# Reordering the first tile: weight chunks against the second batch of keys and values

## The chip, the core and the metric

The kernel runs on one core of a Trainium2 chip. The metric is the device time of the core in microseconds (us), from the start of the program to its end. TensorE is PE in the profile, VectorE DVE, ScalarE ACT, GpSimd POOL; SyncE (SP) issues all transfers.

## What is computed

Three layers follow each other, on 8 batches of 8 heads, 576 positions, 64 dimensions per head, so 4608 tokens of 512 features. The first is a linear attention whose `k`-`v` product is a 64 by 64 matrix per head; the second a feed-forward layer with a rational function; the third a gated one. Cut to what matters here:

```python
kv  = einsum('bhsd,bhse->bhde', k, v)
out = einsum('bhsd,bhde->bhse', q, kv)
x   = out / sqrt(mean(out * out, -1) + 1e-6) * g_norm      # then tokens by 512
h   = x @ w_in                                             # 512 by 2048
g   = (a0 + a1*h + a2*h*h + a3*h*h*h) / (1 + |b0|*|h| + |b1|*h*h + 1e-6)
y   = g @ w_out                                            # 2048 by 512
# third layer: silu(y @ w_gate) * (y @ w_val) @ w_o2
```

All inputs are float32. Products of the two feed-forward layers are made as three matmuls of a high and a low part (`mm3`).

## The kernel before

**Tiles and steps.** Tokens are worked in 9 tiles of 512. In the second layer a tile takes 16 steps (`NF1`), one for each 128 of the 2048 hidden features; step `s` runs over all tiles, `t, f = divmod(s, NF1)`. On PE a step is `h_mm(s)` (12 matmuls, the hidden features of this step, into one of two PSUM banks `ph`), then `y_mm(s - 2)` (12 matmuls, what the step two earlier gives to the output), and now and then a matmul of the attention of the next tile (`attn_pe`: `po` or `ss`).

**The function of a step.** `g_step(s)` reads the bank `ph` with three ACT instructions and three DVE ones (tiles `e`); before its own DVE part it runs `g_finish(s - 1)`, three DVE instructions, after which ACT makes the high part of `ghl` and POOL the low part. `y_mm(s - 1)` waits for these. The bank `ph` of step `s`, which `h_mm(s + 2)` needs again, is free when the last DVE instruction of `g_step(s)` is done. In this document block `s` is what DVE does from the first instruction of `g_finish(s - 1)` to the start of the next block.

**Weight chunks.** In the first tile the 32 chunks of the second layer's weights (512 KB each) are also brought in and converted: 16 of `w_in` (here i0 to i15) and 16 of `w_out` (o0 to o15), in the order i0, i1, i2, o0, i3, o1, i4, o2 and so on, numbered 0 to 31. Chunk `n` ends in a tile `wt` that has the slot `w{n}`. A conversion takes a shift on DVE and a scaling on ACT (`w_scale`, both on `wraw`), a join on DVE, the high part on ACT (`w_hi`) and a subtraction on DVE (`wt<-wraw,wt`). The raw chunks lie in a ring of four tiles, so chunk `n` can be fetched when chunk `n - 4` has had its subtraction. ACT and DVE take their instructions in the order in which they are written, and so does SP with the transfers: an instruction that waits for a chunk holds what is behind it.

**Keys and values.** The 8 batches of keys and values (2.25 MB each, four loads `kvm` and one `kvr`) use slots of the same pool `w` before the `wt` tiles come to them. A batch's products on PE (`kv_mm`, four times) go into the bank `pkv` (`pa1`, there is one) and are copied out by ACT (`kvf` for the first two batches, `kvc` for the others). The first batch is multiplied while the first tile's `x` is made; the second follows, before step 0; the others stand in the steps 0, 3, 4, 7, 8 and 11 of tile 0, one each.

**The first tile before.** Ahead of step 0, chunk 0 is converted alone and chunks 1 and 2 as a pair; each step of tile 0 then converts two:

```python
            g_step(s, raws[:2] if t == 0 else raw_u[0][f - 3:f - 2] if t == TILES - 1 and 3 <= f < 5 else ())
            ...
            if t == 0:
                lows = wa_hi(len(raws[:2]))
                for w in raws[:2]:
                    w_scale(w)
                run(lows, 2)
                wa_fetch(2)
                kv_load(4, done)
```

The order of everything in this stage is written out by hand; no scheduler moves it.

Of the kernel before, what the change touches and what calls it, by code (L numbers as in the profile page):

```python
# [8 lines left out]
F32 = mybir.dt.float32  # L9
# [6 lines left out]
P = 128  # L16
# [7 lines left out]
NF1, NF2 = F1 // P, F2 // P  # L24
HP = H // 2
LAG = 2
WARM = 10
S1 = TILES * NF1
NP = 2
# [11 lines left out]
def fused_kernel(ctx: ExitStack, tc: tile.TileContext, kv_main, kv_left, q_t, w_in, w_out, w_gate, w_val, w_o2, ab, g_norm, out):  # L41
# [48 lines left out]
    def act(out, in_, func=AF.Copy, **kw):  # L90
        nc.scalar.activation(out=out, in_=in_, func=func, **kw)  # L91
# [95 lines left out]
    kv_jobs = [(b, hp) for b in range(B) for hp in range(HP)]  # L187
    kv_last = {}

    def kv_tag(n):  # L190
        slots = (24, 25, 28, 29, 30, 20, 21, 22, 23)
        return f"w{slots[n] if n < 5 else slots[(n - 5) % 9] if n < 28 else slots[n - 27]}"

    def kv_load(k, done=None):

        done = kv_n[1] if done is None else done
        for n in range(kv_n[0], min(kv_n[0] + k, len(kv_jobs))):
            b, hp = kv_jobs[n]
            tag = kv_tag(n)
            if kv_last.get(tag, -1) >= done or (b > 1 and done < n - hp - HP):  # L200
                return
            kv_last[tag] = n
            m = w_p.tile([P, 4, 2, P], F32, tag=tag, name="kvm")
            nc.sync.dma_start(out=m, in_=kv_main[b, hp])
            if hp == 0:
                r = w_p.tile([64, HP, 2, P], F32, tag=("w26", "w27")[b % 2], name="kvr")
                nc.sync.dma_start(out=r, in_=kv_left[b])
                kv_in[b] = r
            kv_in[b, hp] = m
            kv_n[0] += 1  # L210

    def kv_mm(ps):
        b, hp = kv_jobs[kv_n[1]]
        kv_n[1] += 1
        m, r = kv_in.pop((b, hp)), kv_in[b]
        for c in range(4):
            for j in range(2):
                nc.tensor.matmul(ps[diag(j), hp, diag(j)], lhsT=m[:, c, 0, diag(j)], rhs=m[:, c, 1, diag(j)], start=(c == 0), stop=False)
        for j in range(2):
            nc.tensor.matmul(ps[diag(j), hp, diag(j)], lhsT=r[:, hp, 0, diag(j)], rhs=r[:, hp, 1, diag(j)], start=False, stop=True)  # L220

    def diag(j):
        return slice(64 * j, 64 * j + 64)

    def kv_evac_first(b, ps, hps):
        for j in range(2):
            dst, src = kvf[diag(j), b, hps, diag(j)], ps[diag(j), hps, diag(j)]
            act(dst, src)

    def kv_evac(b, ps):  # L230
        for j in range(2):
            act(kvc[diag(j), b - 2, :, :], ps[diag(j), :, diag(j)])

    def kv_split(b):
        hi, lo = kvh[b % 2], kvl[b % 2]
# [170 lines left out]

    def g_step(s, joins=()):
        ps = ew.pop(s)
        attn_head(s)
# [4 lines left out]
        act(e2, ps, AF.Abs, scale=ab_raw[:, 4:5])  # L414
        act(e3, ps, AF.Identity, scale=na[:, 3:4], bias=na[:, 2:3])
# [12 lines left out]
        mid[s] = (e1, e2, e3)  # L428
# [340 lines left out]
    with tc.manual_schedule():  # L769
# [11 lines left out]
            elif i == 2:  # L781
                wa_fetch(1)
        nc.sync.dma_start(out=ab_raw, in_=ab.partition_broadcast(P))
        wa_fetch(1)
        kv_load(1)
        wa_fetch(1)
        nc.vector.memset(kvf, 0.0)
        nc.vector.memset(ones_b, 0.0)
        for j in range(2):
# [11 lines left out]
        def first(i, stage):  # L801
            if not 0 <= i < HP:
                return
            if stage == "kv":
                kv_mm(pkv)
                kv_evac_first(0, pkv, slice(i, i + 1))
                kv_load(1)
            elif stage == "out":
                po[i] = out_mm(0, i, ps_y.tile([P, N], F32, tag=f"y{i}", name="po"))
                sqs[i] = w_p.tile([P, N], F32, tag=f"w{8 + i}", name="sq")  # L810
                act(sqs[i], po[i], AF.Square)
            elif stage == "ss":
                pss[i] = ss_mm(0, sqs[i], ps_h.tile([P, N], F32, tag="ph", name="ss"))
                nb[i] = tuple(w_p.tile([P, N], F32, tag=f"w{k + i}", name="nb") for k in (12, 16))
                norm_start(0, pss[i], nb[i])
            elif stage == "norm":
                st["n"] = nb[i]
                ops = norm_ops(po[i], pss[i])
                run(ops, 3)
            else:  # L820
                st["n"] = nb[i]
                x_attn(0, i, nc.gpsimd)

        for i in range(HP + 2):
            if i == 1:
                nc.vector.tensor_scalar(out=g_neg, in0=g_raw, scalar1=-0.5 / D, scalar2=None, op0=ALU.mult)
            first(i, "kv")
            first(i - 1, "ss")
            first(i, "out")
            if i == 1:  # L830
                w_scale(raws[0])
            elif i == 2:
                w_join(raws[0])
            elif i == 3:
                wa_split(1)
            first(i - 1, "norm")
            first(i - 2, "x")
        nc.vector.tensor_scalar(out=na, in0=ab_raw[:, 0:4], scalar1=-1.0, scalar2=None, op0=ALU.mult)
        act(b_abs, ab_raw[:, 4:6], AF.Abs)
        pkv = ps_a.tile([P, HP, P], F32, tag="pa1", name="pkv")  # L840
        for i in range(HP):
            kv_mm(pkv)
            if i == 0:
                q_load(1, 0)
                wa_fetch(2)
        kv_evac_first(1, pkv, slice(0, HP))
        attn_pe(-1)
        for w in raws[:2]:
            w_scale(w)
        w_join(*raws[:2])  # L850
        lows = wa_hi(2)
        for w in raws[:2]:
            w_scale(w)
        run(lows, 2)
        kv_load(3)
        wa_fetch(2)
        kv_load(2)


        kv_b = None  # L860
        for s in range(S1):
            t, f = divmod(s, NF1)
            if s == S1 - NF1:
                attn_ctx.close()
                late["p"] = ctx.enter_context(tc.tile_pool(name="late", bufs=1, side="right", reuse_waits="tile"))
                u_fetch(0)
                u_fetch(1)
            done = kv_n[1]
            h_mm(s)
            if s >= LAG:  # L870
                y_mm(s - LAG)
            attn_pe(s)
            if t == TILES - 1 and f == 2:
                u_scale(0)
            if kv_b:
                kv_evac(*kv_b)
                kv_b = None
            if t == 0 and f in (0, 3, 4, 7, 8, 11):
                pkv = ps_a.tile([P, HP, P], F32, tag="pa1", name="pkv")
                kv_b = (kv_jobs[kv_n[1]][0], pkv)  # L880
                for _ in range(HP):
                    kv_mm(pkv)
            g_step(s, raws[:2] if t == 0 else raw_u[0][f - 3:f - 2] if t == TILES - 1 and 3 <= f < 5 else ())
            if s >= LAG and f == LAG - 1:
                y_evac((s - LAG) // NF1, s_p, "stg")
            attn_tail(s)
            if t == 0:
                lows = wa_hi(len(raws[:2]))
                for w in raws[:2]:
                    w_scale(w)  # L890
                run(lows, 2)
                wa_fetch(2)
                kv_load(4, done)
            if t == TILES - 1:
                if f == 5:
                    val[0] = [w_views(r)[2] for r in raw_u.pop(0)]
                    u_first(nc.gpsimd)
                elif f in (6, 7):
                    raw_x["D", f - 6] = y_fetch(0, f - 6, 0, N, s_p, "stg")
# [230 lines left out]
```

## Time and profile before

| | |
|---|---|
| time, median of 3 runs | 1732.32 us (1731.52 to 1733.18) |
| time of the profiled execution | 1728.57 us |
| its span, first to last instruction | 1726.8 us |
| PE busy in the span | 1702.2 us (99%) |
| DVE busy in the span | 1227.9 us (71%) |
| ACT busy | 1002.0 us (58%) |
| POOL busy | 460.5 us (27%) |
| HBM read, written | 117.44 MB, 57.67 MB |

Times inside the profile count from the start of the span. The profiled execution's time is 1.8 us above its span and 3.75 us below the median of the timed runs. Matmuls overlap, so the start of one and the start of the next tell more than their durations; "busy" of PE hides nothing but waits.

### The profile page before, as it was taken

The numbers are of one execution on the slowest core, as the hardware profiler recorded it, in microseconds if no ns is written. First come the engines' busy times: TensorE is split into PE (matmuls) and PEld (weight loads), VectorE is DVE, ScalarE is ACT, GpSimd is POOL, SyncE is SP. The second block draws the span as 40 slices with busy tenths as digits, with TensorE's granted clock in tenths as the row PEclk, the third lists the DMA queues.
The fourth block names the chain that finished last, engine by engine and source line by source line (L and its number), as shares of the span: only waits on it lengthen the run. The fifth ranks groups of instructions, "written<-read, shape, count | busy, mean of one in ns | idle before, by whom it ended". The sixth has DMA issues, their size and how long they took to land.

```text
span 1726.8 us, 21854 instructions
## 1 busy us (share of the span) xinstructions
PE 1702.2 (99%) x8112; PEld 1403.0 (81%) x8112; DVE 1227.9 (71%) x1657; ACT 1002.0 (58%) x1664; POOL 460.5 (27%) x331
## 2 busy tenths in 40 slices
PE   8999999999999999999999999999999999999999
PEld 5767888888888888888888888888888888888887
DVE  5989999999999999998886656666547666213211
ACT  6878787878778787877774434444334445112110
POOL 1223444444444343433322302222102212000000
PEclk9999999999999999999999999999999999999999
DMA  9771101000101010001107537222542355423411
GB/s 328 277 232 53 37 13 37 13 31 13 37 13 37 13 38 13 31 13 52 71 31 270 199 110 274 80 91 81 189 152 99 109 193 199 169 98 132 161 49 49
DMA packets 68682, 176.53 MB, mean 102 GB/s; under 512 B 7648, under 2 KB 10208, under 8 KB 66784
## 3 DMA queue, kind: packets, MB, share of 16 engines
q1 hardware_dynamic: 68576, 175.15, 28.8%
q8 instruction: 63, 1.03, 0.3%
q14 instruction: 43, 0.35, 0.1%
HBM read 117.44 MB, written 57.67 MB: 101 GB/s over the span
## 4 chain that ended last, share of the span: by engine, by line
PE 52%; issue 1%; DVE 0%; DMA 0%; POOL 0%; ACT 0%; SPq 0%; DVEq 0%; POOLq 0%; ACTq 0%
PE pb L105 10%; PE pb L106 10%; PE pb L107 10%; PE pb L757 6%; PE pb L759 6%; PE pb L758 6%; PE y L107 1%; PE y L105 1%; PE y L106 1%; PE ph L106 1%; PE ph L107 1%; PE ph L105 1%; DVE e L432 0%; DMA yraw<-yd 0%; POOL xc L94 0%
## 5 line engine op out<-in xcount | busy, mean ns | idle before, releaser
L94 POOL TENSOR_TENSOR ghl<-e,ghl 128x512 fp32r<-128x512 f32 x144 | 192.9, 1340 | 517.3 <-ACT ghl L91 229.0
L105 PE MATMUL pb<-xc,wu 128*128 128x512 f32 (+1 forms) x816 | 308.9, 378 | 1.1 <-DVE e L432 1.1
L106 PE MATMUL pb<-xc,wu 128*128 128x512 f32 (+1 forms) x816 | 308.6, 378 | 0.0
L107 PE MATMUL pb<-xc,wu 128*128 128x512 f32 (+1 forms) x816 | 308.6, 378 | 0.0
L101 DVE SCALAR_TENSOR_TENSOR e<-e,e 128x512 f32<-128x512 f32 x288 | 247.3, 859 | 30.8 <-ACT e L91 24.6
L106 PE MATMUL y<-ghl,wt 128*128 128x512 f32 x576 | 226.4, 393 | 6.3 <-POOL ghl L94 6.3
L105 PE MATMUL ph<-x,wt 128*128 128x512 f32 x576 | 227.8, 396 | 0.0
L105 PE MATMUL y<-ghl,wt 128*128 128x512 f32 x576 | 225.5, 391 | 2.3 <-ACT ghl L91 2.3
L107 PE MATMUL y<-ghl,wt 128*128 128x512 f32 x576 | 225.8, 392 | 0.0
L106 PE MATMUL ph<-x,wt 128*128 128x512 f32 x576 | 225.3, 391 | 0.1
L107 PE MATMUL ph<-x,wt 128*128 128x512 f32 x576 | 224.6, 390 | 0.0
L432 DVE TENSOR_TENSOR e<-e,pb 128x512 f32<-128x512 f32 (+1 forms) x192 | 124.5, 653 | 139.5 <-PE pb L107 85.4
L91 ACT ACTIVATE e<-pb 128x512 f32<-128x512 f32 (+1 forms) x144 | 82.2, 571 | 233.2 <-PE pb L107 232.9
L105 PEld LDWEIGHTS pb<-xc,wu 128*128 128x128 f32 x816 | 153.3, 188 | 30.4 <-DVE e L432 1.7
L107 PEld LDWEIGHTS pb<-xc,wu 128*128 128x128 f32 x816 | 153.3, 188 | 28.7
L106 PEld LDWEIGHTS pb<-xc,wu 128*128 128x128 f32 x816 | 153.3, 188 | 28.6
L757 PE MATMUL pb<-wo,xc 128*128 128x512 f32 x432 | 168.0, 389 | 0.0
L758 PE MATMUL pb<-wo,xc 128*128 128x512 f32 x432 | 168.0, 389 | 0.0
L759 PE MATMUL pb<-wo,xc 128*128 128x512 f32 x432 | 168.0, 389 | 0.0
L91 ACT ACTIVATE e<-ph 128x512 f32<-128x512 f32 x144 | 85.5, 594 | 117.2 <-PE ph L107 116.9
L378 DVE COPY sb<-pb 128x512 f32<-128x512 f32 x18 | 12.5, 692 | 197.9 <-PE pb L759 197.8
L101 DVE SCALAR_TENSOR_TENSOR e<-e,na,e 128x512 f32<-128x512 f32 x144 | 143.7, 998 | 0.0
(120 smaller groups left out, 3057.8 us busy)
## 6 DMA issues: line engine op xcount, KB each, us to landing
graw<-gd SPq DMA_DIRECT2D x108, 256.0 KB, 4.8
gd<-gout SPq DMA_DIRECT2D x84, 256.0 KB, 2.0
kvm<-in_kv_main SPq DMA_DIRECT2D x32, 512.0 KB, 9.3
yraw<-yd SPq DMA_DIRECT2D x26, 512.0 KB, 6.0
q<-in_q_t SPq DMA_DIRECT2D x36, 256.0 KB, 2.7
yd<-sb SPq DMA_DIRECT2D x18, 512.0 KB, 3.3
wraw<-in_w_in SPq DMA_DIRECT2D x16, 512.0 KB, 6.1
wraw<-in_w_out SPq DMA_DIRECT2D x16, 512.0 KB, 3.9
```

The costliest lines, as they stand in the source:

```text
L91: nc.scalar.activation(out=out, in_=in_, func=func, **kw)
L94: eng.tensor_tensor(out=out, in0=a, in1=b.bitcast(F32), op=ALU.subtract)
L101: nc.vector.scalar_tensor_tensor(out=out, in0=in0, scalar=scalar, in1=in1, op0=op0, op1=op1)
L105: nc.tensor.matmul(ps, lhsT=wh, rhs=xh, start=first, stop=False, skip_group_check=more)
L106: nc.tensor.matmul(ps, lhsT=wh, rhs=xl, start=False, stop=False, skip_group_check=more)
L107: nc.tensor.matmul(ps, lhsT=wl, rhs=xh, start=False, stop=last, skip_group_check=more)
L378: nc.vector.tensor_copy(out=sb[:, 1, :], in_=yps[2 * j + 1])
L432: eng.tensor_tensor(out=out, in0=a, in1=b, op=op)
L757: nc.tensor.matmul(b[m], lhsT=gh, rhs=w[:, 0, :], start=f == 0, stop=False)
L758: nc.tensor.matmul(b[m], lhsT=gh, rhs=w[:, 1, :], start=False, stop=False)
L759: nc.tensor.matmul(b[m], lhsT=gl, rhs=w[:, 0, :], start=False, stop=f == NF2 - 1)
```

## The change

Ahead of step 0 five chunks are converted instead of three, one at a time (`convert`), and their transfers are issued ahead of the second batch's. The products of the second batch are moved behind `h_mm(0)`, and the first attention matmuls of the second tile move one or two steps back. The batch that was multiplied in step 0 is multiplied in step 3; each later batch moves on by one place, and step 7 takes two (`kv_batches(2)`), copied out by one instruction. The function `pace` sets how many chunks a step converts: one in the steps 1, 2, 5 and 6, three in 8 and 9, two in the others. The transfer slots of keys and values are listed in a new table (`kv_slots`) in place of `kv_tag`.

```diff
+PRE = 5
-    def kv_evac(b, ps):
-        for j in range(2):
-            act(kvc[diag(j), b - 2, :, :], ps[diag(j), :, diag(j)])
+    def kv_batches(k):
+        ps = ps_a.tile([P, 2, HP, D], F32, tag="pa1", name="pkv")
+        b = kv_jobs[kv_n[1]][0]
+        for i in range(k):
+            for _ in range(HP):
+                kv_mm(lambda hp, j: ps[diag(j), i, hp, :])
+        return partial(act, kvc[:, b - 2:b - 2 + k, :, :], ps[:, :k])
...
-        wa_fetch(1)
+        wa_fetch(3)
         kv_load(1)
-        wa_fetch(1)
...
+        def convert():
+            w_scale(raws[0])
+            w_join(raws[0])
+            wa_split(1)
+            wa_fetch(1)
...
             elif i == 3:
                 wa_split(1)
+                wa_fetch(1)
+                q_load(1, 0)
             first(i - 1, "norm")
             first(i - 2, "x")
+            if i > 3:
+                convert()
...
-        pkv = ps_a.tile([P, HP, P], F32, tag="pa1", name="pkv")
-        for i in range(HP):
-            kv_mm(pkv)
-            if i == 0:
-                q_load(1, 0)
-                wa_fetch(2)
-        kv_evac_first(1, pkv, slice(0, HP))
-        attn_pe(-1)
+        for _ in range(PRE - 3):
+            convert()
         for w in raws[:2]:
             w_scale(w)
-        w_join(*raws[:2])
-        lows = wa_hi(2)
-        for w in raws[:2]:
-            w_scale(w)
-        run(lows, 2)
-        kv_load(3)
-        wa_fetch(2)
-        kv_load(2)
+        def pace(s):
+            return 1 if s in (1, 2, 5, 6) else 3 if s in (8, 9) else 2
+        scaled = 2
...
             h_mm(s)
+            if s in (1, 2):
+                attn_pe(2 * s - 3)
             if s >= LAG:
                 y_mm(s - LAG)
-            attn_pe(s)
+            if s == 0:
+                pkv = ps_a.tile([P, HP, P], F32, tag="pa1", name="pkv")
+                for _ in range(HP):
+                    kv_mm(kv_first(pkv))
+                kv_evac_first(1, pkv, slice(0, HP))
+                done = kv_n[1]
+            elif s > 2:
+                attn_pe(s)
...
-            if t == 0 and f in (0, 3, 4, 7, 8, 11):
-                pkv = ps_a.tile([P, HP, P], F32, tag="pa1", name="pkv")
-                kv_b = (kv_jobs[kv_n[1]][0], pkv)
-                for _ in range(HP):
-                    kv_mm(pkv)
-            g_step(s, raws[:2] if t == 0 else raw_u[0][f - 3:f - 2] if t == TILES - 1 and 3 <= f < 5 else ())
+            if t == 0 and f in (3, 4, 7, 8, 11):
+                kv_b = kv_batches(2 if f == 7 else 1)
+            if t == 0:
+                for w in raws[scaled:pace(s)]:
+                    w_scale(w)
+            g_step(s, raws[:pace(s)] if t == 0 else raw_u[0][f - 3:f - 2] if t == TILES - 1 and 3 <= f < 5 else ())
...
-                lows = wa_hi(len(raws[:2]))
-                for w in raws[:2]:
+                lows = wa_hi(len(raws[:pace(s)]))
+                k = len(lows)
+                scaled = min(len(raws), pace(s + 1))
+                for w in raws[:scaled]:
                     w_scale(w)
-                run(lows, 2)
-                wa_fetch(2)
+                run(lows, k)
+                wa_fetch(k)
+                attn_tail(s)
                 kv_load(4, done)
```

PE at the end of the first tile's attention, before: the last two of the second batch's four groups of products (`pkv`), the next tile's `po`, and then the first product of step 0 (`ph`).

```order
L218 MATMUL pkv<-kvm 64x64 x8
L220 MATMUL pkv<-kvr 64x64 x2
L218 MATMUL pkv<-kvm 64x64 x8
L220 MATMUL pkv<-kvr 64x64 x2
L256 MATMUL po<-q,kvf 128x64
L256 MATMUL po<-q,kvf 128x448
L105 MATMUL ph<-x,wt 128x512
```

And now, the same place:

```order
L267 MATMUL po<-q,kvf 128x512
L287 MATMUL ss<-sq,ones_b 128x512
L106 MATMUL ph<-x,wt 128x512
L107 MATMUL ph<-x,wt 128x512
L108 MATMUL ph<-x,wt 128x512
```

Step 0 follows the first tile's last `ss` at once; the second batch's products come behind its 12 matmuls, and `po` behind those of step 1.

DVE from the last instruction of the first tile's norm (`nb`) to the first of step 0 (`e`), before; `x2` is a pair of chunks:

```order
L101 SCALAR_TENSOR_TENSOR nb<-po,g_neg,nb 128x512
L838 TENSOR_SCALAR na<-ab_raw 128x4
L125 TENSOR_SCALAR wraw<-wraw 128x512 x2
L101 SCALAR_TENSOR_TENSOR wraw<-wraw 128x512 x2
L125 TENSOR_SCALAR wraw<-wraw 128x512 x2
L94 TENSOR_TENSOR wt<-wraw,wt 128x512 x2
L101 SCALAR_TENSOR_TENSOR wraw<-wraw 128x512 x2
L101 SCALAR_TENSOR_TENSOR e_559<-e_559,b_abs,e_560 128x512
```

And now, the last of the four single conversions and what follows it:

```order
L126 TENSOR_SCALAR wraw<-wraw 128x512
L102 SCALAR_TENSOR_TENSOR wraw<-wraw 128x512
L95 TENSOR_TENSOR wt<-wraw,wt 128x512
L126 TENSOR_SCALAR wraw<-wraw 128x512 x2
L102 SCALAR_TENSOR_TENSOR wraw<-wraw 128x512 x2
L102 SCALAR_TENSOR_TENSOR e_517<-e_517,b_abs,e_518 128x512
```

Between the norm and step 0 stood one pair of conversions (chunks 1 and 2) with the shifts and joins of a second pair; there are now four whole conversions, one behind the other (chunks 1 to 4), and then the shifts and joins of chunks 5 and 6.

DVE between the step 9 and the step 10, now (`wt<-` x3 are the subtractions of chunks 20, 21 and 22):

```order
L126 TENSOR_SCALAR wraw<-wraw 128x512
L95 TENSOR_TENSOR wt<-wraw,wt 128x512 x3
L126 TENSOR_SCALAR wraw<-wraw 128x512
L102 SCALAR_TENSOR_TENSOR e_1313<-e_1313,e_1314 128x512
L102 SCALAR_TENSOR_TENSOR e_1315<-e_1315,na,e_1314 128x512
L102 SCALAR_TENSOR_TENSOR wraw<-wraw 128x512
L102 SCALAR_TENSOR_TENSOR e_1315<-e_1313,e_1315 128x512
```

The shift behind the three subtractions is that of chunk 24, and it stands ahead of `g_finish(9)`. Before the change both shifts of a block stood ahead of its subtractions, and nothing stood between these and the next `g_finish`.

## Rows read from the trace of the kernel before

**Rows 1.** Stretches: busy us of each engine (instructions), PEclk (granted clock), DMA share, GB/s.
```profile
0.00:30.00 30.00, 21.61 (x201) 13.37 (x202) 15.90 (x30) 17.90 (x36) 7.78 (x12) 0.97 0.93 321
30.00:160.00 130.00, 118.81 (x869) 91.67 (x868) 118.30 (x192) 105.92 (x184) 31.20 (x23) 0.97 0.65 222
160.00:1726.80 1566.80, 1561.78 (x7046) 1297.90 (x7044) 1093.68 (x1435) 878.19 (x1445) 421.53 (x297) 1.00 0.25 88
```
**Rows 2.** Waits of PE from 0 to 200 us: total us, times, longest.
```profile
PE y L106 <- POOL ghl L94: 6.3, 6, 1.8
PE pkv L218 <- DMA kvm<-in_kv_main: 3.7, 7, 1.3
PE y L105 <- ACT ghl L91: 2.3, 3, 0.9
```
**Rows 3.** Timeline of DVE, blocks 5 and 6: start us, us, instruction, [idle before].
```profile
72.33 0.69 DVE L101 SCALAR_TENSOR_TENSOR e<-e,e 128x512 f32<-128x512 f32 x1
74.19 0.69 DVE L101 SCALAR_TENSOR_TENSOR e<-e,e 128x512 f32<-128x512 f32 x1
78.18 1.29 DVE L94 TENSOR_TENSOR wt<-wraw,wt 128x512 fp32r<-128x512 f32 x2
79.39 0.69 DVE L101 SCALAR_TENSOR_TENSOR e<-e,e 128x512 f32<-128x512 f32 x1
```
**Rows 4.** Timeline of DVE: the norm's last instruction, and step 0.
```profile
23.57 0.75 DVE L101 SCALAR_TENSOR_TENSOR nb<-po,g_neg,nb 128x512 f32<-128x512 f32 x1
...
34.93 0.75 DVE L101 SCALAR_TENSOR_TENSOR e<-e,b_abs,e 128x512 f32<-128x512 f32 x1 [1.53 <-ACT e L91]
...
36.32 0.75 DVE L101 SCALAR_TENSOR_TENSOR e<-e,na,ph 128x512 f32<-128x512 f32 x1
```
**Rows 5.** Timeline of ACT there: high parts of two chunks.
```profile
27.56 1.27 ACT L91 ACTIVATE wt<-wraw 128x512 fp32r<-128x512 f32 x2 [0.20 <-DVE wraw L101]
```
**Rows 6.** Timeline of POOL: the first low part of `ghl`.
```profile
43.40 1.65 POOL L94 TENSOR_TENSOR ghl<-e,ghl 128x512 fp32r<-128x512 f32 x1 [16.92 <-ACT ghl L91]
```
**Rows 7.** Timeline of PE: step 3 begins; `y_mm(6)`; products of step 8; step 9.
```profile
47.77 0.39 PE L105 MATMUL ph<-x,wt 128*128 128x512 f32 x1
...
95.66 0.39 PE L105 MATMUL y<-ghl,wt 128*128 128x512 f32 x1
...
99.91 0.69 PE L218 MATMUL pkv<-kvm 128*64 128x64 f32 x16 [1.36 <-ACT kvc L91]
...
103.41 0.50 PE L105 MATMUL ph<-x,wt 128*128 128x512 f32 x1
```
**Rows 8.** Waits of PE from 47.8 to 95.6 us, all.
```profile
PE y L106 <- POOL ghl L94: 2.4, 2, 1.5
PE y L105 <- ACT ghl L91: 0.5, 1, 0.5
```
**Rows 9.** The stretch of `y_mm(9)`, columns as in rows 1.
```profile
120.40:124.00 3.60, 3.56 (x9) 2.85 (x10) 3.60 (x7) 3.00 (x6) 0.00 (x0) 0.53 1.05 218
```
**Rows 10.** Transfers issued from 98 to 114 us: size, median us from issue to landing.
```profile
wraw<-in_w_out SPq DMA_DIRECT2D x2, 512.0 KB, 3.5
wraw<-in_w_in SPq DMA_DIRECT2D x2, 512.0 KB, 4.3
```
**Rows 11.** Transfers issued from 0 to 60 us, columns as in rows 10.
```profile
wraw<-in_w_in SPq DMA_DIRECT2D x8, 512.0 KB, 6.9
```
**Rows 12.** Timeline of DVE: blocks 10, 11 and 12 begin, two waits ahead of block 12.
```profile
115.49 0.68 DVE L101 SCALAR_TENSOR_TENSOR e<-e,e 128x512 f32<-128x512 f32 x1
...
125.25 0.68 DVE L101 SCALAR_TENSOR_TENSOR e<-e,e 128x512 f32<-128x512 f32 x1
130.92 0.82 DVE L125 TENSOR_SCALAR wraw<-wraw 128x512 int32<-128x512 int32 x1 [0.47 <-DMA wraw<-in_w_out]
132.21 0.43 DVE L125 TENSOR_SCALAR wraw<-wraw 128x512 int32<-128x512 int32 x1 [0.46 <-DMA wraw<-in_w_in]
133.75 0.69 DVE L101 SCALAR_TENSOR_TENSOR e<-e,e 128x512 f32<-128x512 f32 x1
```

More of the change, by code (lines that the diff above doesn't have):

```diff
@@ L188, in fused_kernel @@
     kv_last = {}
-    def kv_tag(n):
-        slots = (24, 25, 28, 29, 30, 20, 21, 22, 23)
-        return f"w{slots[n] if n < 5 else slots[(n - 5) % 9] if n < 28 else slots[n - 27]}"
+    kv_slots = [(24, 25, 28, 29, 26), (30, 24, 25, 28, 27), (29, 20, 21, 22, 26), (23, 17, 18, 19, 27)]
+    kv_slots += [(30, 24, 25, 28, 16), (29, 20, 21, 22, 26), (23, 17, 18, 19, 27), (30, 25, 28, 29, 26)]
     def kv_load(k, done=None):
@@ L198, in kv_load @@
             b, hp = kv_jobs[n]
-            tag = kv_tag(n)
-            if kv_last.get(tag, -1) >= done or (b > 1 and done < n - hp - HP):
+            tag, rest = f"w{kv_slots[b][hp]}", f"w{kv_slots[b][HP]}"
+            if kv_last.get(tag, -1) >= done or (hp == 0 and kv_last.get(rest, -1) >= done):
                 return
@@ L205, in kv_load @@
             if hp == 0:
-                r = w_p.tile([64, HP, 2, P], F32, tag=("w26", "w27")[b % 2], name="kvr")
+                kv_last[rest] = n + HP - 1
+                r = w_p.tile([64, HP, 2, P], F32, tag=rest, name="kvr")
                 nc.sync.dma_start(out=r, in_=kv_left[b])
@@ L217, in kv_mm, with kv_first @@
             for j in range(2):
-                nc.tensor.matmul(ps[diag(j), hp, diag(j)], lhsT=m[:, c, 0, diag(j)], rhs=m[:, c, 1, diag(j)], start=(c == 0), stop=False)
+                nc.tensor.matmul(ps(hp, j), lhsT=m[:, c, 0, diag(j)], rhs=m[:, c, 1, diag(j)], start=(c == 0), stop=False)
         for j in range(2):
-            nc.tensor.matmul(ps[diag(j), hp, diag(j)], lhsT=r[:, hp, 0, diag(j)], rhs=r[:, hp, 1, diag(j)], start=False, stop=True)
+            nc.tensor.matmul(ps(hp, j), lhsT=r[:, hp, 0, diag(j)], rhs=r[:, hp, 1, diag(j)], start=False, stop=True)
     def diag(j):
         return slice(64 * j, 64 * j + 64)
+    def kv_first(ps):
+        return lambda hp, j: ps[diag(j), hp, diag(j)]
     def kv_evac_first(b, ps, hps):
@@ L408, in g_step @@
         ps = ew.pop(s)
-        attn_head(s)
+        if s > 1:
+            attn_head(s)
         e1 = e_p.tile([P, N], F32, tag="e1", name="e1")
@@ L414, in g_step @@
         act(e2, ps, AF.Abs, scale=ab_raw[:, 4:5])
+        if s == 1:
+            attn_head(0)
         act(e3, ps, AF.Identity, scale=na[:, 3:4], bias=na[:, 2:3])
@@ L869, in fused_kernel @@
             h_mm(s)
+            if s in (1, 2):
+                attn_pe(2 * s - 3)
             if s >= LAG:
                 y_mm(s - LAG)
-            attn_pe(s)
+            if s == 0:
+                pkv = ps_a.tile([P, HP, P], F32, tag="pa1", name="pkv")
+                for _ in range(HP):
+                    kv_mm(kv_first(pkv))
+                kv_evac_first(1, pkv, slice(0, HP))
+                done = kv_n[1]
+            elif s > 2:
+                attn_pe(s)
             if t == TILES - 1 and f == 2:
@@ L875, in fused_kernel @@
             if kv_b:
-                kv_evac(*kv_b)
+                kv_b()
                 kv_b = None
-            if t == 0 and f in (0, 3, 4, 7, 8, 11):
-                pkv = ps_a.tile([P, HP, P], F32, tag="pa1", name="pkv")
-                kv_b = (kv_jobs[kv_n[1]][0], pkv)
-                for _ in range(HP):
-                    kv_mm(pkv)
-            g_step(s, raws[:2] if t == 0 else raw_u[0][f - 3:f - 2] if t == TILES - 1 and 3 <= f < 5 else ())
+            if t == 0 and f in (3, 4, 7, 8, 11):
[4 more added lines that the diff above has]
+            g_step(s, raws[:pace(s)] if t == 0 else raw_u[0][f - 3:f - 2] if t == TILES - 1 and 3 <= f < 5 else ())
             if s >= LAG and f == LAG - 1:
                 y_evac((s - LAG) // NF1, s_p, "stg")
-            attn_tail(s)
-            if t == 0:
-                lows = wa_hi(len(raws[:2]))
-                for w in raws[:2]:
+            if t:
+                attn_tail(s)
+            else:
+                lows = wa_hi(len(raws[:pace(s)]))
+                k = len(lows)
+                scaled = min(len(raws), pace(s + 1))
+                for w in raws[:scaled]:
                     w_scale(w)
-                run(lows, 2)
-                wa_fetch(2)
+                run(lows, k)
+                wa_fetch(k)
+                attn_tail(s)
                 kv_load(4, done)
```

## The prediction

> **What bounds the kernel now.** I read first the stretches, then the waits of PE, then the timelines of DVE and PE in the first tile. From 160 us on PE is busy for 1561.8 of 1566.8 us, and the change touches nothing there [rows 1]. All that can be won lies ahead of 160 us: PE waits for the two parts of `ghl` for 8.6 us and for key and value loads for 3.7 [rows 2]. Behind these waits stands DVE: from 30 to 160 us it is busy for 118.3 of 130 us, or 91%, as much as PE with 118.8 [rows 1]. A plain block of DVE with two conversions takes 7.06 us (72.33 to 79.39, [rows 3]); the 24 matmuls of a plain step take less, the steps with a batch of products take more, so that now the one and now the other waits. Evening this out is worth at most the waits; the question is whether the new order does it.
>
> **The change, part by part.** I follow one chain through the first tile, in times of the profiled execution, and compare where the work done is equal.
>
> *Ahead of step 0.* Before, the norm ends at 24.3 us, and the first `e` of step 0 starts on DVE at 34.93 [rows 4]. Now four conversions stand there, one at a time. Each passes from DVE (shift 0.43, [rows 12]; join 0.69, as a DVE instruction of this size takes in [rows 3]) to ACT (0.64, half of [rows 5]) and back to DVE (0.65, half of a pair in [rows 3]), 2.4 us and about 0.1 for the passes: 10 us, to 34.3. Then two shifts and two joins, 2.1: the first `e` at 36.4 to 36.9 (ACT, with two scalings and two copies of `kvf` ahead of its own `e`, is ready at the later end); I take 36.7, **1.8 us later** than before. The loads are no obstacle by their volume: all that is asked for up to chunk 6 is 10.5 MB, at 321 GB/s [rows 1] landed by 32.7 us. `h_mm(0)` itself comes earlier, no longer behind the second batch's products, but neither engine that reads its bank is free earlier.
>
> *To the end of `y_mm(0)`.* From the first `e` to the end of the third takes 2.1 us (34.93 to 37.07, [rows 4]); one shift and two subtractions 1.8; then the four instructions of `g_finish(0)` with its join 2.5 (72.33 to 74.88, [rows 3]); ACT's high part 0.65, POOL's low part 1.65 [rows 6]: 45.4 us. Eleven of the 12 matmuls of `y_mm(0)` follow, 2.7 of the 2.9 us that such a product takes (95.66 to 98.55, [rows 7]): 48.1 instead of 47.77. PE has waited twice by then, for the bank of `h_mm(2)` until 38.8 and for `ghl`. In the row of `y_mm(9)`, behind two waits, the granted clock was 0.53 for 3.6 us, which cost 1.7 us [rows 9]; here it may cost 0 to 1.7, and I take half, 0.9: 49.0.
>
> *From there to the end of `h_mm(8)`.* Before, this took 47.9 us (47.77 to 95.66, [rows 7]), 2.9 of them waits [rows 8], so 45.0 of work. Now PE has one batch more to do in it, the one taken out of step 0, at 3.5 us (99.91 to 103.41, [rows 7]), and hardly a wait: blocks 1, 2, 5 and 6, with one conversion, are 1.55 us shorter each (0.43, 0.69 and 0.65, less 0.08 each by which neighbours overlap: 78.18 + 1.29 against 79.39, [rows 3]), and the batches come where DVE can use the time. `h_mm(8)` ends at 49.0 + 45.0 + 3.5 + 0.2 = 97.7, against 95.66: **2.0 us later, with the same products done**. What the front lost here came back only as far as the waits of [rows 8]. Then `y_mm(6)`, 2.7, to 100.4; the products of step 8 no longer wait 1.36 us for the copy of the previous batch [rows 7], and step 9 starts at 103.9 instead of 103.41.
>
> *Steps 8 to 10.* Here the order has a weak place. The ring holds four raw chunks, and a step that converts three leaves one in it. So the second and third chunk of step 9 (21 and 22) and the second of step 10 (24) are fetched only by the subtractions of the block before, and their shifts stand ahead of `g_finish`, which `y_mm` waits for. Step 8's chunks 17 to 19 go into the slots w17 to w19, which its batch frees with the second, third and fourth quarter of its 3.5 us, at 102.2, 103.0 and 103.9. High part and subtraction behind these bring the subtractions to their end at 103.5, 104.1 and 105.3. Chunk 21 is issued at 103.5, 22 at 104.1; an unhurried load takes 3.5 us, the second of a pair 4.3 [rows 10], so 22 lands at 108.4, is shifted by 108.8, and `g_finish(8)` starts there, not at 106.0 (105.3 and two shifts): 2.8 us lost. Block 9 with three conversions takes 7.06 + 1.55 less a shift, 8.2, to 117.0. Chunk 24 is fetched when the first of its three subtractions ends, at 115.8, lands at 119.3 and is shifted by 119.65: another 2.3 us lost. The last batch's loads (2.25 MB) are done by then.
>
> The Trainium skill ("DMA: Bandwidth & Descriptors", section "Anatomy of one DMA") gives for a transfer a fixed cost of some 2.0 us and the bytes at 436 GB/s, and says that the fixed part does not shrink. It speaks against this change, since a chunk fetched by the block before cannot come in less; by its figures a chunk would take an estimated 3.2 us and the two waits 2.5 and 2.0 us, 0.6 less in the sum.
>
> *From block 10 on* the work is the same in both. Before, block 10 starts at 115.49, now at 119.65, 4.15 later. Before, block 12 waits twice for chunks, 0.93, and one shift is drawn out by 0.4 [rows 12], because the last batch's loads are in their way; these loads now go out ahead, so 1.4 comes back. **Sum: 4.15 - 1.4 = +2.7 us**, on DVE up to the last conversion, and by `ghl` on PE; from 160 us on PE carries it to the end unchanged.
>
> **How it could go otherwise.** *Faster: the loads of steps 9 and 10 hold nobody.* If the two waits are hidden, because PE reaches step 9 later than DVE anyway or chunks land sooner, 5.1 us go away, and with the clock's 0.9 the sum is -3.3; if the four conversions also run into each other as pairs did, the 1.8 of the front goes too: -5.1, or 1727.2 us. For it speak the waits of [rows 2], which are there to be won; against it that `g_finish(8)` stands behind both shifts in the order of DVE, and that 3.5 us is the shortest kind of landing [rows 10]. It decides at a landing below some 1.5 us behind the block's last subtraction.
>
> *Slower: step 0 waits for chunk 6.* DVE and ACT take the shift and scaling of chunks 5 and 6 before the first `e`. Chunk 6 can be issued only after chunk 2's subtraction, at 29.3 us, and in the first 60 us such a load took 6.9 us [rows 11]: landing at 36.2, and the first `e` 2.0 us later than I have it. PE has no wait left up to step 8 that could take this in, so +4.7: 1737.0. It decides from a landing later than 34.3 on; against it stands the volume above.
>
> *The change only moves the waits.* DVE has the same instructions in all, and if it stays the bound from 35 us on, the new order gives what the old one gave: 1732.3. For it speaks the 91%, against it that five conversions have left the steps.
>
> **How the numbers follow.** The profiled execution took 1728.57 us, 3.75 below the median of the timed runs. With +2.7 it becomes 1731.3, and the median 1735.0, my forecast. Its own parts leave 3 us on either side (clock 0 to 1.7, pitch of the conversions, where the slots come free), 1732 to 1738. A measurement of this kernel tells some 0.2% (3.5 us) from no change, so faster means below 1728.9 and slower above 1735.8. Chances: the forecast's chain 0.55 (same 0.34, slower 0.21); the loads hidden 0.22 (faster 0.17, same 0.05); step 0 held 0.15 (slower 0.14, same 0.01); waits only moved 0.08 (same). Together faster 0.17, same 0.48, slower 0.35. The range, 1727 to 1741, takes in both rivals' times and the clock's upper end on the slower one.
>
> **What the new profile would show.** The first `e` of step 0 on DVE near 36.7 and `y_mm(0)` ending near 49; hardly a PE wait from there to 97; then DVE idle for loads of chunks just ahead of `g_finish(8)` and `g_finish(9)`, some 5 us together, and PE waiting over 4 us for `ghl` in `y_mm(9)`. If the first `e` comes at 35, or if those two idle times are missing, the prediction is too slow; if `pkv` products in steps 3 to 8 wait for loads or for ACT's copies, too fast. A PE wait behind 170 us would mean that the change reaches further than I think.

## The result, and the profile after

The changed kernel takes 1744.6 us against 1731.1 of the kernel before, medians of runs on one chip: ratio 1.0077, 95% interval 1.0066 to 1.0088. One of its six runs, at a granted clock of 0.85 (0.99 in the others), took 1898.75 us and is left out. It is slower by 13.5 us; the forecast was 1735.0 us and a range up to 1741. The profiled execution took 1746.9 us, its span is 1745.1, 18.3 more than before; this is more than 13.5 because it lies 2.3 us above its median and the profiled execution of before, with 1728.57, 2.6 us below. At its start PE waits 1.1 us for a load of keys and values (`kvr`), and the first `e` of step 0 comes at 40.26, in the traces of the experiments with the same front at 38.0 to 39.9.

The stretches of the changed kernel, which answer to [rows 1] (columns as there):

```profile
30.00:160.00 130.00, 113.73 (x885) 86.84 (x886) 105.75 (x173) 91.61 (x158) 25.21 (x18) 0.90 0.67 223
160.00:1745.10 1585.10, 1576.75 (x7103) 1309.20 (x7101) 1110.66 (x1458) 891.01 (x1468) 427.55 (x302) 1.00 0.25 87
```

From 30 to 160 us both engines that bound the kernel do less than before in the same time: PE 113.7 us for 118.8, DVE 105.8 for 118.3. Behind 160 us PE is idle for 8.4 us, before for 5.0. Part of it is new: PE waits 0.6 and 1.6 us for `x` of the second tile, at 176.99 and 179.06, where the kernel before has no wait. From step 12 to step 18 both still take the same, 40.9 and 40.8 us, so what is lost is lost ahead of step 12.

The waits of PE up to 200 us, which answer to [rows 2], and those of DVE from 24 to 180 us (total us, times, longest):

```profile
PE y L106 <- ACT ghl L92: 7.5, 3, 5.0
PE y L107 <- POOL ghl L95: 6.4, 6, 1.5
PE ph L107 <- POOL x L95: 3.4, 3, 1.6
...
DVE wraw L126 <- DMA wraw<-in_w_in: 13.5, 4, 5.6
...
DVE wraw L126 <- DMA wraw<-in_w_out: 5.1, 2, 3.0
```

PE waits 1.1 us for key and value loads instead of 3.7, but 14 us for `ghl`; and DVE, which makes `ghl`, waits six times for raw chunks, 18.6 us together. In the kernel before the same two rows add to 9.1:

```profile
DVE wraw L125 <- DMA wraw<-in_w_in: 5.5, 6, 1.7
DVE wraw L125 <- DMA wraw<-in_w_out: 3.6, 4, 1.4
```

The timeline of DVE in the changed kernel shows the six waits and, behind four of them, the `g_finish` that they hold (start us, us, instruction, [idle before]):

```profile
67.54 0.43 DVE L126 TENSOR_SCALAR wraw<-wraw 128x512 int32<-128x512 int32 x1 [3.42 <-DMA wraw<-in_w_in]
...
69.09 0.68 DVE L102 SCALAR_TENSOR_TENSOR e<-e,e 128x512 f32<-128x512 f32 x1
...
101.65 0.43 DVE L126 TENSOR_SCALAR wraw<-wraw 128x512 int32<-128x512 int32 x1 [5.65 <-DMA wraw<-in_w_in]
...
106.32 0.43 DVE L126 TENSOR_SCALAR wraw<-wraw 128x512 int32<-128x512 int32 x1 [3.04 <-DMA wraw<-in_w_out]
106.66 0.68 DVE L102 SCALAR_TENSOR_TENSOR e<-e,e 128x512 f32<-128x512 f32 x1
...
118.05 0.43 DVE L126 TENSOR_SCALAR wraw<-wraw 128x512 int32<-128x512 int32 x1 [2.03 <-DMA wraw<-in_w_out]
120.72 0.43 DVE L126 TENSOR_SCALAR wraw<-wraw 128x512 int32<-128x512 int32 x1 [2.24 <-DMA wraw<-in_w_in]
121.06 0.68 DVE L102 SCALAR_TENSOR_TENSOR e<-e,e 128x512 f32<-128x512 f32 x1
...
132.59 0.43 DVE L126 TENSOR_SCALAR wraw<-wraw 128x512 int32<-128x512 int32 x1 [2.18 <-DMA wraw<-in_w_in]
132.94 0.69 DVE L102 SCALAR_TENSOR_TENSOR e<-e,e 128x512 f32<-128x512 f32 x1
```

In order these are the chunks 12 (in block 3, where its shift is made ahead for step 4), 18 and 19 (at the end of block 7, for step 8), 21, 22 and 24. The last three are the waits of the prediction, 6.5 us instead of 5.1. The first three, 12.1 us, are not in it: `g_finish(8)` starts at 121.06, the prediction had 108.8, and block 10 at 132.94 instead of 119.65 (before 115.49, [rows 12]).

Why chunk 18 came so late is told by the transfers: those issued from 76.5 to 89 us, the one at 90.0, and the pair at 102.7 and 103.3 (size, median us from issue to landing):

```profile
kvm<-in_kv_main SPq DMA_DIRECT2D x8, 512.0 KB, 11.5
...
wraw<-in_w_out SPq DMA_DIRECT2D x1, 512.0 KB, 12.0
...
wraw<-in_w_in SPq DMA_DIRECT2D x1, 512.0 KB, 11.6
...
wraw<-in_w_out SPq DMA_DIRECT2D x1, 512.0 KB, 3.5
wraw<-in_w_in SPq DMA_DIRECT2D x1, 512.0 KB, 5.5
```

Chunk 18 was issued at 90.0 us with the loads of two batches still under way, and took 11.6 us; without such company the same transfer takes 3.5. And because its shift stands on DVE ahead of the subtractions that free the ring, chunks 19 and 20 could only be issued at 102.7.

The Trainium skill ("DMA: Bandwidth & Descriptors", section "Anatomy of one DMA") fits a transfer that GpSimd issues by 2.0 us and the bytes at 436 GB/s, for 512 KB an estimated 3.2 us. These loads are issued by SP; the one that met no other comes near it with 3.5 us.

PE's wait for the high part of `ghl` at the place of [rows 9], now 5 us long, and the stretch around it (columns as in [rows 1]):

```profile
136.80 0.79 PE L106 MATMUL y<-ghl,wt 128*128 128x512 f32 x1 [4.97 <-ACT ghl L92]
139.14 0.80 PE L107 MATMUL y<-ghl,wt 128*128 128x512 f32 x1 [1.54 <-POOL ghl L95]
```

```profile
136.00:144.00 8.00, 5.65 (x12) 4.09 (x13) 8.00 (x15) 6.13 (x11) 2.21 (x1) 0.50 0.22 78
```

The granted clock is 0.50 there, the lower level of 1.2 GHz; in the kernel before, whose PE is busy throughout from 136 to 144 us, it is 1.00.

### The profile page after: what moved, and what is told of

Its sections match the earlier page's. It is cut to its first block, busy times and chain, and to the rows that moved or that the text cites. A ratio compares the mean times of both kernels' runs of the same rounds, so it can differ in the third digit from the quotient of the medians.

```text
span 1745.1 us, 21855 instructions
## 1 busy us (share of the span) xinstructions
PE 1711.5 (98%) x8112; PEld 1407.9 (81%) x8112; DVE 1231.6 (71%) x1657; ACT 998.0 (57%) x1657; POOL 460.4 (26%) x331
## 4 chain that ended last, share of the span: by engine, by line
PE 51%; issue 1%; DVE 0%; DMA 0%; POOL 0%; ACT 0%; SPq 0%; DVEq 0%; POOLq 0%; ACTq 0%
PE pb L106 10%; PE pb L107 10%; PE pb L108 10%; PE pb L771 6%; PE pb L773 6%; PE pb L772 6%; PE y L106 1%; PE y L107 1%; PE y L108 1%; PE ph L107 1%; PE ph L108 1%; PE ph L106 1%; DVE e L446 0%; DMA yraw<-yd 0%; POOL xc L95 0%
```

## The experiments

Ratios are against the kernel before, run on the same chip, with 95% intervals. The theory after the result was: late chunk loads cost what the prediction lacks. Its rivals: the dearer start, or PE itself (the moved products, and the lower clock behind its waits).

**A fifth raw chunk, `e1_ring5`** (at the start one chunk more is asked for).

```diff
-    wa_raw = ((at_p, "hl"), (at_p, "r0"), (s_p, "stg"), (s_p, "stg"))
+    wa_raw = ((at_p, "hl"), (at_p, "r0"), (s_p, "stg"), (s_p, "stg"), (at_p, "r1"))
...
-            w_fetch(*wa_raw[n % 4], wa_src[n][2])
+            w_fetch(*wa_raw[n % 5], wa_src[n][2])
```

> The changed kernel with a ring of five raw chunks instead of four, one chunk fetched earlier at the start, nothing else. Loads theory (the loss lies in raw chunks that land late: chunks 18, 19, 21, 22 and 24 hold DVE for 5.65 + 3.04 + 2.03 + 2.24 + 2.18 us): chunks 19, 21 and 24 are now fetched one block earlier and 18 ahead of the seventh batch's loads, so 8 to 13 us come back, ratio 1.000 to 1.003. Start theory (the loss lies in the conversions ahead of step 0, first e 5.3 us later, and PE carries it to the end): no more than 1 us comes back, ratio 1.007. PE theory (the moved products and the half clock behind PE's waits): as the start theory.

Measured: 1731.7 us, 1.0011 (1.0001 to 1.0020). All but 0.11% came back, with only two waits left and `g_finish(8)` and block 10 where the prediction had them within 0.6 and 2.1 us:

```profile
94.73 0.43 DVE L126 TENSOR_SCALAR wraw<-wraw 128x512 int32<-128x512 int32 x1 [2.13 <-DMA wraw<-in_w_out]
...
107.91 0.43 DVE L126 TENSOR_SCALAR wraw<-wraw 128x512 int32<-128x512 int32 x1 [1.69 <-DMA wraw<-in_w_in]
108.25 0.69 DVE L102 SCALAR_TENSOR_TENSOR e<-e,e 128x512 f32<-128x512 f32 x1
...
117.56 0.69 DVE L102 SCALAR_TENSOR_TENSOR e<-e,e 128x512 f32<-128x512 f32 x1
```

**Two conversions in the steps 8 and 9, `e2_pace2`** (`3 if s in (8, 9)` taken out of `pace`).

> The changed kernel with two chunks in the steps 8 and 9 instead of three; the last chunk is converted in step 15. Loads theory: no shift stands ahead of g_finish any more, the waits for 19, 21, 22 and 24 go (9.5 us), those for 12 and 18 stay; 7 to 10 us come back, ratio 1.002 to 1.004. Start theory: nothing comes back, ratio 1.007 to 1.008. A third possibility: the last chunks come too late for PE in the steps 14 to 17, ratio above 1.008.

Measured: 1736.0, 1.0029 (1.0018 to 1.0040). The waits for 19, 21 and 22 went, 23 and 24 wait 1.5 and 0.8 us, 12 and 18 as before (3.5 and 3.4); PE now waits for weight tiles that come too late (`y` for `wt`, 5.8 and 3.1 us).

**The batch's loads not behind step 5, `e3_kvlate`** (`if s != 5:` ahead of `kv_load(4, done)`).

> The changed kernel without the load of a batch at the end of step 5; that batch is loaded at the end of step 6, behind chunk 18. Loads theory: the 5.65 us of DVE for chunk 18 go, and chunk 19, fetched behind it, comes earlier: 4 to 7 us back, ratio 1.004 to 1.006. Ring theory alone (only the ring's depth counts, not what is ahead in SP's queue): nothing comes back, 1.0077. Risk: the batch's products in step 8 wait for their loads instead, PE idle there 1 to 3 us.

Measured: 1740.9, 1.0065 (1.0049 to 1.0080). Chunk 18 no longer waits, but chunk 19 does, 4.65 us, behind the same loads a step later. The wait moves.

**The conversions of the start in pairs, `e4_pairs`.**

```diff
-            w_scale(raws[0])
-            w_join(raws[0])
-            wa_split(1)
-            wa_fetch(1)
+            for w in raws[:2]:
+                w_scale(w)
+            w_join(*raws[:2])
+            run(wa_hi(2), 2)
+            wa_fetch(2)
```

> The changed kernel with the four conversions ahead of step 0 made as two pairs behind the first tile's x instead of four singles. Start theory: the first e of step 0 comes 2 to 4 us earlier and all of it reaches the end, ratio 1.005 to 1.0065. Loads theory: the first e is as early, but DVE then waits longer for chunks 12 and 18, whose loads PE and SP set, and under 1 us reaches the end, ratio 1.007 to 1.008.

Measured: 1745.0, 1.0079 (1.0058 to 1.0101). Nothing came back. But the first `e` hardly came earlier (38.4 us), since DVE now waited 2.6 us for the load of chunk 4: the run does not show what an earlier start would be worth.

**A fifth raw chunk in the kernel before, `e5_before_ring5`** (as e1; the fetch behind the second batch's first products asks for three).

> The kernel before with a fifth raw chunk and nothing else. Theory 'the changed order makes the chunk loads late': the kernel before has little to win, its waits of DVE for raw chunks are 7.2 us in all up to 180 us and PE waits for few of them; 1729 to 1731 us, ratio 0.998 to 1.000. Rival 'a ring of four is simply too short, whatever the order': it gains as much as the changed kernel did, some 11 us, 1720 us.

Measured: 1726.2, 0.9970 (0.9957 to 0.9983). More than expected: a fifth chunk is worth some 5 us in the kernel before too. With equal rings the new order is still 0.41% behind (1.0011 against 0.9970), some 7 us.

**The rest of batch 2, the third (batches are counted from 0), asked for ahead of step 0, `e6_early`** (`kv_load(4)` before the first step), **and with a fifth raw chunk, `e7_early_ring5`.**

> The changed kernel with the four loads of the third batch asked for ahead of step 0, as far ahead as the kernel before had them, and not at the end of step 0. Theory 'the removed early loads left the transfers idle from 30 to 50 us (share 0.73 and 0.58, before 0.98 and 0.90, that is 5.7 us) and the same bytes then stood in the way of chunks 12, 18 and 19': the waits of DVE for these chunks (3.4, 5.7 and 3.0 us) fall by half or more, and the time falls by 7 to 10 us to 1734 to 1737. Rival 'the fetch behind the block's own subtraction costs it, with or without the batches': the waits at 101 to 106 us move by less than a microsecond, and the time stays at 1742 to 1745.

> The changed kernel with both, the early loads of the third batch and a fifth raw chunk. Theory of the loads: the last 3.8 us of DVE waiting for chunks that the ring alone left (2.1 at 94.7, 1.7 at 107.9) mostly go, 1728 to 1730 us, just below the kernel before. Rival 'what is left after the ring is no matter of loads, but of DVE, which is 92% busy to 160 us': as the ring alone, 1731 to 1732.

Measured: 1744.9, 1.0074 (1.0059 to 1.0089), and 1731.8, 1.0005 (0.9995 to 1.0014). A miss. The transfers were busier early (share 0.83 from 30 to 50 us, 0.65 in the changed kernel), but chunks 18 and 19 still waited 3.6 and 4.4 us: the loads of batches 5 and 6 (the sixth and seventh) still go out from 75 to 86 us, when the products of the steps 3 and 4 have freed their slots.

**Three chunks at the start, `e8_front3`** (`PRE = 3`, two conversions in the steps 1 and 2).

> The changed kernel with three chunks converted ahead of step 0 and two in the steps 1 and 2, so that from step 3 on as many chunks are done as now; the second batch stays behind step 0. Theory 'the dearer front is paid back by the lighter steps 1 and 2' (three steps in, the first e is 0.4 us later than in the kernel before, while it was 5.3 late in step 0): the first e of step 0 comes 5 to 6 us earlier, but at step 3 it stands where it does now, within 1.5 us, and the time stays at 1742 to 1746. Rival 'the four conversions one behind the other cost 3.6 us that never come back': 1739 to 1741.

Measured: 1744.0, 1.0071 (1.0054 to 1.0087). The time is as the first theory says, but the start did not get shorter, so that the run does not price it: the first `e` came at 37.26, hardly earlier, since ACT copies the second batch ahead of its own `e` and waits for these products until 35.26:

```profile
35.26 0.77 ACT L92 ACTIVATE kvf<-pkv 64x256 f32<-64x256 f32 x2 [3.49 <-PE pkv L223]
```

**A fifth raw chunk and two conversions in the steps 8 and 9, `e9_ring5_pace2`.**

> The changed kernel with a fifth raw chunk and two conversions, not three, in the steps 8 and 9. With a fifth raw chunk the kernel before is still some 5.4 us ahead of the changed one; up to step 7 the changed one leads by 2.4 us, and it loses 7.1 in the steps 7 to 10. Theory 'the two further conversions in the steps 8 and 9 cost there what DVE has no room for (1.55 us each) and bring the last two waits for chunks (2.1 and 1.7 us)': 1727 to 1729 us. Rival 'put off, they are too late for PE' (with a ring of four PE then waited 5.8 and 3.1 us for weight tiles): 1731 to 1734.

Measured: 1731.3, 0.9998 (0.9986 to 1.0009). The waits for chunks are gone (0.4 us), those for weight tiles are there (3.2 and 2.5): the conversions taken from the steps 8 and 9 are missing later.

**The chunks on another queue, `e10_poolq` and `e11_actq`.**

```diff
-                wa_fetch(k)
+                wa_fetch(k, nc.gpsimd)
```

(`nc.scalar` in e11; `w_fetch` issues on the engine that it is given.)

> The changed kernel with the chunks of the steps asked for by POOL on a queue of its own, the ring of four and all batches as they are. In the changed kernel chunk 18 was asked for at 90.0 us, behind nine loads of two batches on SP's queue, and landed 11.6 us later. Theory 'it stands behind these loads because one queue is served in order': on its own queue it lands within 4 to 7 us of its issue, DVE's waits of 5.7 and 3.0 us go for the most part, and the time is 1733 to 1738. Rival 'the transfer engines are simply full until 100 us, whatever the queue': landing still 10 us or more after the issue, 1742 to 1746.

> As the run with POOL's queue, but the chunks of the steps are asked for by ACT. Theory of the one queue: landing 4 to 7 us after the issue, the waits for chunks 18 and 19 mostly gone; ACT, however, waits for the subtractions of DVE before each issue, at most 1 us in a step, so 1733 to 1740. Rival of the full engines: landing 10 us or more, 1742 to 1748.

Measured: 1742.7, 1.0066 (1.0043 to 1.0090), and 1741.5, 1.0058 (1.0041 to 1.0076). The rival is nearer. On its own queue chunk 18 did land in 3.6 us, but SP, which no longer stops for the ring, sent the batches ahead, and chunks issued between 65 and 82 us were as slow as ever:

```profile
kvm<-in_kv_main SPq DMA_DIRECT2D x6, 512.0 KB, 14.5
wraw<-in_w_out POOLq DMA_DIRECT2D x2, 512.0 KB, 9.5
wraw<-in_w_in POOLq DMA_DIRECT2D x2, 512.0 KB, 11.2
```

In e10 DVE still waits 17.7 us for chunks. Some 7 us of it, for the chunks 12 and 13, stand behind such slow loads; the other 10.4, for 19, 21, 22 and 24, come with loads that landed in 3.4 to 4.7 us and were only asked for too late, by their own block's subtractions. So another queue alone cures neither; nor is this a clean test of the queue, since the wait for the ring now holds up POOL or ACT, which have other work to do.

**A quarter of the bytes, a ring of four and of five, both orders: `e12_quarter`, `e13_quarter_ring5`, `e14_before_quarter_ring5`, `e15_before_quarter`.**

```diff
-            nc.sync.dma_start(out=m, in_=kv_main[b, hp])
+            if b > 1:
+                nc.sync.dma_start(out=m[:, 0:1], in_=kv_main[b, hp][:, 0:1])
+            else:
+                nc.sync.dma_start(out=m, in_=kv_main[b, hp])
```

> The changed kernel with a quarter of the bytes in the key and value loads of the batches 2 to 7: each load brings the first of its four parts, and the products use that part four times, so that PE, ACT, DVE and POOL do as much as now. The output is that of other keys and values. Theory 'the batches' bytes stand in the way': DVE's waits for chunks 12, 18 and 19 (3.4, 5.7 and 3.0 us) go, those for 21, 22 and 24 (2.0, 2.2 and 2.2) stay, and the time is 1732 to 1737. Rival 'the ring of four by itself, each fetch behind the block's own subtraction': three or four waits of 2 to 4 us stay in the steps 7 to 10, and the time is 1739 or more.

> As e12, with a fifth raw chunk too: no chunk should be late. Theory 'what is behind after the ring is still the loads' (3.8 us of waits were left): 1726 to 1728, level with e14. Rival 'the order itself costs DVE time': 1730 to 1732, still some 4 us behind e14.

> The kernel before with a fifth raw chunk and the same quarter of the bytes in the loads of the batches 2 to 7 (the output is that of other keys and values). With all the bytes it took 1726.2 and waited 3 to 5 us for chunks, mostly behind PE's own pace: 1724 to 1727.

> The kernel before with its ring of four and the quarter of the bytes (the output is that of other keys and values). It gained 4.9 us by a fifth raw chunk. Theory 'there too the batches' bytes made the chunks late': as much by fewer bytes, 1725 to 1728. Rival 'there the ring by itself was short': 1729 to 1731.

Measured: e12 1736.9, 1.0039 (1.0024 to 1.0054); e13 1733.0, 1.0012 (1.0002 to 1.0023); e14 1724.9, 0.9969 (0.9958 to 0.9980); e15 1724.4, 0.9964 (0.9953 to 0.9976). In the order of before, fewer bytes alone or a longer ring alone give all that both together give. In the new order the bytes give 0.38%, and another 0.27% needs the fifth chunk: a fetch behind a block's own subtraction comes too late by itself (with few bytes chunks 12 and 18 no longer wait, but 19, 21, 22 and 24 do, 2.7, 1.7, 2.0 and 2.1 us). And e13 shows the second half of the loss: with nearly no late chunk, the new order is 8.0 us behind the old one. The stretches of e13 and, behind them, of e14 say where (columns as in [rows 1]):

```profile
60.00:100.00 40.00, 40.00 (x403) 32.20 (x402) 36.73 (x59) 30.72 (x53) 10.16 (x7) 1.00 0.50 158
100.00:124.00 24.00, 21.05 (x154) 16.29 (x152) 20.46 (x31) 18.33 (x33) 5.77 (x5) 1.00 0.58 175
```

```profile
60.00:100.00 40.00, 40.00 (x362) 31.72 (x358) 38.28 (x63) 34.49 (x62) 10.45 (x7) 1.00 0.51 167
100.00:124.00 24.00, 24.00 (x210) 19.00 (x210) 23.21 (x37) 20.35 (x36) 5.88 (x5) 1.00 0.49 157
```

Up to 100 us PE has no gap in either; DVE has less to do in the new order and waits. From 100 to 124 us PE runs through in the old order and waits 3.0 us in the new. The timeline of DVE in e13 has two of its waits:

```profile
100.84 0.75 DVE L102 SCALAR_TENSOR_TENSOR e<-e,b_abs,e 128x512 f32<-128x512 f32 x1 [2.26 <-ACT e L92]
...
108.73 0.43 DVE L126 TENSOR_SCALAR wraw<-wraw 128x512 int32<-128x512 int32 x1 [1.73 <-DMA wraw<-in_w_in]
```

The first `e` of step 8 waits because `h_mm(8)` stands behind the double batch of step 7, 80 matmuls from 89.56 to 96.57 us; then DVE makes three conversions each in two blocks. By the first `e` of the steps 7 and 10, 89.63 and 123.13 in e13, 92.52 and 116.96 in e14, a lead of 2.9 us becomes a lag of 6.2. At step 7 this is not a lead in work: by then the new order has made two conversions and a batch of products less, and both come between the two times. At step 10 the same is done in both.

**Less of the double batch, `e16_short_batch`** (e13, and of the second batch in step 7 only the first 8 of 40 matmuls).

> As e13 (ring of five, a quarter of the bytes), and of the second batch in step 7 only 8 of 40 matmuls are made, 2.8 us of PE less (the output is that of other keys and values). Theory 'PE has no slack from 60 to 100 us, and the double batch makes the first e of step 8 wait (2.3 us)': that wait goes, and the time falls by 2 to 3 us, to 1730 to 1731. Rival 'DVE with its three conversions in the steps 8 and 9 sets the pace in any case': 1732 to 1733, as e13.

Measured: 1730.1, 0.9991 (0.9982 to 1.0001), 0.21% or some 3.6 us less than e13 by the ratios, and the wait ahead of the first `e` of step 8 is gone. The matmuls left out are 2.8 us of PE, which either order has to make. So the run shows that PE's time in step 7 goes straight into the whole; it does not show that the double batch costs more there than two batches in two steps.

## Why the prediction was wrong

**The step that failed** is "Steps 8 to 10". Its premise is that step 8's three subtractions wait for nothing but their slots w17 to w19, and so end at 103.5, 104.1 and 105.3; the sum has no term for the loads of the chunks 18 and 19. In the changed kernel DVE waits 5.7 and 3.0 us for these two ahead of step 8's first `e`, and the three subtractions begin only at 114.13:

```profile
114.13 1.90 DVE L95 TENSOR_TENSOR wt<-wraw,wt 128x512 fp32r<-128x512 f32 x3 [0.29 <-ACT wt L92]
```

So `g_finish(8)` starts 12.3 us and block 10 13.3 us later than forecast. I had reckoned the loads by volume at the start and by their landing time in the steps 9 and 10, and not at all in between, where the loads of batches 5 and 6 now stand.

The part before it, "to the end of `h_mm(8)` ... hardly a wait", held on PE: from `y_mm(0)` to there the changed kernel took 49.7 us (51.50 to 101.18), the forecast 48.7, though DVE waited 3.4 us for chunk 12 in it. What was off there came from the start.

**What e1 shows, and what in it is luck.** With the fifth chunk block 10 starts within 2.1 us of the forecast, and the span is 2.8 us over that of before, where I had +2.7. The way there is not the forecast's, though. Of the 5.1 us that my sum counts for the chunks 21, 22 and 24, 1.7 is left in e1 (and 2.1 for chunk 19); in place of the others stands a lag of the order itself: PE begins `y_mm(6)` at 98.64, 3.0 us later than before.

**What was right by steps.** The weak place of the steps 8 to 10 was there, in the changed kernel: 4.3 us for chunks 21 and 22 (2.8 forecast), 2.2 for 24 (2.3), and 5.0 us of PE waiting in `y_mm(9)`. With chunks 18 and 19 in time (e1) step 8's subtractions end at some 104.4, 105.3 and 106.2, near the forecast's 103.5, 104.1 and 105.3. And neither chunk 6 nor another load held step 0.

**Sizes and smaller steps.** The first `e` came at 38.0 to 39.9 us in the traces that share this front (40.26 in the changed kernel), not at 36.7: the subtractions of e13 stand at 27.44, 31.09, 33.74 and 36.29, 2.6 to 3.7 us apart, not 2.5. `y_mm(0)` ended 2.5 us later than forecast, little beside the 13.3 us of block 10. The 0.9 us for the clock measured next to nothing: the granted clock was 0.50 from 32 to 40 us, but 1.00 from 44 to 52, and the matmuls of `y_mm(0)` behind its last wait stand 0.23 us apart. The 1.4 us expected back behind block 10 did not come back (block 10 starts 17.5 us later than before, the span is 18.3 longer), and the sign set for a change that reaches further, a PE wait behind 170 us, did appear. The rival "waits only moved" was given little because "five conversions have left the steps"; only two have, for three stood ahead of step 0 already.

On DVE the front's loss did come back by step 3 (the first `e` there at 60.71, before 60.36). On PE it did not. With the same products done, `y_mm(6)` begins in e13 and, behind it, in e14, the two orders with a fifth chunk and few bytes, at:

```profile
99.43 0.39 PE L106 MATMUL y<-ghl,wt 128*128 128x512 f32 x1
```

```profile
97.01 0.39 PE L105 MATMUL y<-ghl,wt 128*128 128x512 f32 x1
```

That is 2.4 us later, where the prediction had 2.0 for this place.

**The sign of the order itself was wrong.** Without the 5.1 us for new waits and the 1.4 for old ones, my sum left -1.0 us for the order itself. With loads nearly out of the way it is +7.4 (1.0012 against 0.9969; the spans differ by 8.4). PE in e13 and e14 shows where. The 2.4 us of `y_mm(6)` are still 2.4 when step 11 begins (117.67 and 115.25). Then `y_mm(9)` waits twice in e13, and not in e14:

```profile
123.21 0.49 PE L106 MATMUL y<-ghl,wt 128*128 128x512 f32 x1 [2.65 <-ACT ghl L92]
...
125.04 0.63 PE L107 MATMUL y<-ghl,wt 128*128 128x512 f32 x1 [1.34 <-POOL ghl L95]
```

Behind these waits the granted clock is 0.66 from 124 to 128 us, in e14 it is 1.00 over the same products (117 to 126), and step 12 begins 8.5 us later than in e14 (133.83 and 125.36). Behind step 12 nothing more is lost. `g_finish(9)`, for which PE waits there, is 5.1 us late. On DVE three things stand ahead of it: two conversions more in the blocks 8 and 9 (3.1 us at the 1.55 of the prediction), a wait for a chunk (1.7), and the wait for step 8's `e` (2.3), which goes with the lag that PE already has and is hardly a further loss. I had counted on the lighter steps 5 and 6, but PE, without a gap from 60 to 100 us, could not use the lead of DVE.

That leaves +5.9 of the 13.3 us (0.77%) for the loads: they cost the new order 11.3 us (1.0077 less 1.0012) and the old one 5.4 (1 less 0.9969).

What stays open: the ring and the bytes together explain the loads' share, but how it divides between them depends on which is taken away first (e1 and e7 against e12 and e13). The order's own part is read from two traces; no run changed the start alone, and none the steps 7 to 10 alone, with late loads out of the way.

## What to carry to other kernels

When work is reordered, follow the loads through every step, not only through those whose order looks tight: list what is issued ahead of each urgent transfer and when its buffer comes free. When a wait moves to another chunk, step or queue and the time hardly changes, its cause is still there; here one more buffer was worth more than any order tried, 11 us in the new and 5 us in the old, and the kernel before with a fifth raw chunk (0.9970) beats both. Work taken from a step helps only if the other engine has room in that step. And compare two orders at places where the same work is done: a lead in the middle can be work put off.

## What was not expected of the hardware

**DVE and POOL.** Single DVE instructions take 0.5 to 1.1 us longer than others of their kind: 16 of them in e13 from 20 to 200 us, and at each a subtraction on POOL was running. Three on DVE, and POOL at the same times:

```profile
28.05 1.51 DVE L126 TENSOR_SCALAR wraw<-wraw 128x512 int32<-128x512 int32 x1
...
119.64 1.23 DVE L102 SCALAR_TENSOR_TENSOR wraw<-wraw 128x512 int32<-128x512 int32 x1
120.79 1.21 DVE L102 SCALAR_TENSOR_TENSOR e<-e,e 128x512 f32<-128x512 f32 x1
```

```profile
28.01 1.27 POOL L95 TENSOR_TENSOR x<-nb,x 128x512 fp32r<-128x512 f32 x1 [2.38 <-ACT x L92]
...
119.16 2.29 POOL L95 TENSOR_TENSOR kvl<-kvf,kvh 64x256 fp32r<-64x256 f32 x2 [5.19 <-ACT kvh L92]
```

A shift takes 1.51 us instead of 0.43, a join 1.23 instead of 0.69. The Trainium skill ("SBUF — State Buffer", section "Who interferes with whom") says that a DVE instruction with two inputs in SBUF, or in a two-port mode, and a GpSimd instruction that reads SBUF hold a shared pair of ports against each other; the joins agree with it, and of the shifts, which have one input, these runs do not show the mode.
